# Which weight columns two early FFN products read, and waits for earlier stores on SyncE, in a gated mix of linear attention and a SwiGLU FFN

## The chip, the cores and the metric

The kernel runs on one core of one Trainium2 chip. The metric is the device time of an execution in microseconds (us). It is a little longer (1.2 to 1.8 us in the fast runs here) than the span that the profile shows, which goes from the first to the last instruction of the program on the core; how much longer turns out to matter here. A ratio is the mean time of one kernel's fast runs over that of the other kernel's fast runs of the same rounds, so it is not quite the ratio of the medians.

Names used below: PE is TensorE (matmuls), PEld its weight loads, DVE is VectorE, ACT is ScalarE, POOL is GpSimd, SyncE (SP) issues most DMAs. In the profile a line like L294 is a line of the kernel's text, usually that of a helper.

## The reference, cut to what matters

```python
# x: 2048 tokens x 640, bf16
g = sigmoid((x * gate_w).sum(-1, keepdims=True))
a = linear_attention(x, wqkv, w_phi, wo)      # 32 heads of 20, softmax features of q and k
b = (silu(x @ w_gate) * (x @ w_up)) @ w_down  # w_gate, w_up: 640 x 1728
return g * a + (1 - g) * b
```

The part under study is `x @ w_gate` and `x @ w_up`. The kernel computes them in products for 512 tokens and 128 of the 1728 columns.

## The kernel before

A long list of items, each a small unit of work, fixes the order in which every engine gets its instructions. `F0.8` is the FFN product for tokens 0 to 511 and columns 1024 to 1151 (column block 8). `K`, `V`, `Q` are projections of one tile of 128 tokens, `E` accumulates keys times values, `M` and `R` make projection weights, `D` is one output tile of 128 tokens, with its store. A tracker adds the semaphore waits that the reads and writes need.

```python
LOADS = """
x0 w0 x1 w1 x2 w2 x3 w3 w4 f0 h k0 k1 t4 k2 k3 k4 t5 ... t15 q0 q1 q2 q3
q4 f1 f2
"""
ORDER = """
... M1 i3 M0 F0.0 M2 V4 M3 M4 K0 K1 ...
R2 E5 K9 S8 P7 R1 E6 K10 S9 V12 P8 E7 P9 K11 S10 P10 F0.8 R3 F1.10 E8 E9 K12 E10 S11 S12 K14 S14
V11 K13 P11 P12 E11 K15 P14 R4 S13 P13 F1.9 S15 P15 E12 V13 T F1.8 ...
"""

FCUT = [0, 256, 896, F_FFN]      # columns of the three FFN loads f0, f1, f2

def load_ffn(c0, c1):            # all on SyncE's queue
    dma("sp", wg[:, :, c0:c1], B_w_gate[:, c0:c1].rearrange("(c p) j -> p c j", p=P))
    dma("sp", wu[:, :, c0:c1], B_w_up[:, c0:c1].rearrange("(c p) j -> p c j", p=P))

def fitem(bt, k):                # the FFN product: ten matmuls, one set of waits
    # ... (cut)
        mm(group(g, [(wg[:, c, P * k:P * k + P], xr[c]) for c in range(5)])
           + group(up, [(wu[:, c, P * k:P * k + P], xr[c]) for c in range(5)]))
    # ... (cut: ScalarE, VectorE and GpSimd make silu(gate) * up of it)

def ditem(bt, u):                # an output tile
    # ... (cut: 38 matmuls)
    o = osb[:, t % 4, :]
    if t < NT - 1:
        mm([p for ab in zip(*half) for p in ab])
        actop(o.rearrange("p (b c) -> p b c", b=2), halves(pr), ACTF.Copy, omg[:, t:t + 1])
        out_evs.append(dma("sp", out2[t * P:(t + 1) * P, :], o))
        return
    # ... (cut: the last tile goes out in three stores, two from SyncE and one from ScalarE)
# after the last item:
tr._wait("sp", dict(out_evs))    # SyncE waits until the stores have landed
```

The softmax here doesn't subtract the row's maximum and nothing guards it: scores larger than these inputs give would overflow.

## Time and profile before

| | before |
|---|---|
| time, median of the first 3 runs | 290.0 us (289.88 to 290.5) |
| span of the profiled run | 288.9 us |
| PE busy | 99% of the span |
| starts of back-to-back matmuls of 512 columns | 216 ns apart |

Back-to-back starts were 215.81 ns apart on average for 512 columns and 135.84 ns for 320 columns in this trace: 0.4165 ns a column, or N / 2.4 ns for N columns, and 2.5 ns besides. Start-to-start times less N / 2.4 ns give the holes in PE's stream.

The page of the kernel before. Each engine has its busy time, its share of the span and its number of instructions. The second line is a DMA queue that the page labels "instruction": number of packets within the span, MB, share of the DMA engines. The third is the chain of work that ended last, by engine.

```profile
PE 284.7 (99%) x1975; PEld 174.2 (60%) x1975; DVE 162.6 (56%) x243; ACT 148.1 (51%) x252; POOL 160.5 (56%) x125
...
q14 instruction: 6, 0.05, 0.1%
...
PE 93%; SPq 4%; DMA 2%; issue 0%; DVE 0%
```

PE is the bound: it is almost never idle and nearly all of the last chain is its own. The other engines matter only where PE waits for them.

The chain of waits of the kernel before, in order of time: start, length (us), what.

```profile
11.78 4.92 DMA wT<-in_A_wqkv_dram
...
16.75 34.89 PE ps L294 x344
51.64 0.58 issue
52.22 26.60 PE ps L294 x240
...
128.98 158.03 PE ps L294 x1020
...
287.03 0.32 DVE osb L719
```

The chain is PE work with few interruptions. The largest after the first 17 us is 0.58 us of "issue" at 51.64, which means: the profile does not see what PE waited for.

The timeline of PE around it: start, length (us), the merged instructions, and in brackets the idle time before them.

```profile
50.12 1.52 PE L294 MATMUL ps<-wqk,xT 128*128 128x320 bf16 x10
52.22 1.24 PE L294 MATMUL ps<-xT,wg 128*128 128x512 bf16 x5 [0.58 <-issue]
53.30 1.03 PE L294 MATMUL ps<-xT,wu 128*128 128x512 bf16 x4
```

PE stopped after a key projection (`K11`) and started again at 52.22 with the gate half of an FFN product, `F0.8`. A back-to-back start would have been at 51.47 (start of the last matmul of `K11`, 51.34, plus the 0.135 us that such matmuls of 320 columns are apart), so the hole is 0.75 us.

To find the cause, take the loads that `F0.8` needs. SyncE's timeline of the kernel before has the issues of the second and then the third FFN load (start, length):

```profile
37.70 0.58 SPq L348 DMA_DIRECT2D wg<-in_B_w_gate_dram  x1
38.33 0.52 SPq L348 DMA_DIRECT2D wu<-in_B_w_up_dram  x1
38.89 0.53 SPq L348 DMA_DIRECT2D wg<-in_B_w_gate_dram  x1
39.45 2.13 SPq L348 DMA_DIRECT2D wu<-in_B_w_up_dram  x1
```

The DMA view of the same kernel gives sizes and the time from issue to landing in us:

```profile
wg<-in_B_w_gate_dram SPq DMA_DIRECT2D x1, 1040.0 KB, 10.5
wu<-in_B_w_up_dram SPq DMA_DIRECT2D x1, 1040.0 KB, 12.7
wg<-in_B_w_gate_dram SPq DMA_DIRECT2D x1, 800.0 KB, 6.6
wu<-in_B_w_up_dram SPq DMA_DIRECT2D x1, 800.0 KB, 8.2
```

The 1040 KB loads are the third ones. Adding 39.45 and 12.7 puts the landing of the up half at 52.13 (the unrounded trace), which is 0.06 us before PE's first weight load and 0.09 us before its first matmul. The second load's up half landed at 38.33 + 8.2, or 46.57.

### The profile page before, as it was taken

Reading aid. Unit: us, or ns where it says so; the run is one execution under the profiler, and the core shown is the slowest. Engines: PE = TensorE matmul, PEld = TensorE weight load, DVE = VectorE, ACT = ScalarE, POOL = GpSimd, SP = SyncE. Lnnn points to the kernel's source line nnn. Section 1 sums busy time; section 2 is a strip of 40 time slices with the busy share of each in tenths; the row PEclk is TensorE's granted clock in tenths of the full one; section 3 lists DMA queues with packets and bytes.
Section 4 is the critical chain, followed back from the end, with each engine's and each line's share of the span. In section 5 each row is a group of like instructions: output and inputs, shape, how many; then the busy total and the mean of one; then the engine's idle time right before and its main releaser. Section 6 shows DMA issues by size and latency. Waiting matters only on the chain.

```text
span 288.9 us, 4883 instructions
## 1 busy us (share of the span) xinstructions
PE 284.7 (99%) x1975; PEld 174.2 (60%) x1975; DVE 162.6 (56%) x243; ACT 148.1 (51%) x252; POOL 160.5 (56%) x125
## 2 busy tenths in 40 slices
PE   7999999999999999999999999999999999999997
PEld 6667777575644445556775546675554446656776
DVE  2147748386468987769992285980316799200000
ACT  1478768576674556574354663224675452234112
POOL 8286899779544798844733347450663649601000
PEclk9999999999999999999999999999999999999999
DMA  7988689000010497302373102061020004410101
GB/s 216 173 121 129 119 230 338 7 2 1 0 49 0 75 331 133 71 11 40 63 133 93 20 1 50 2 133 58 2 50 0 2 1 82 93 45 0 48 23 48
DMA packets 48942, 21.61 MB, mean 75 GB/s; under 512 B 39384, under 2 KB 48792, under 8 KB 48920
## 3 DMA queue, kind: packets, MB, share of 16 engines
q1 hardware_dynamic: 48190, 20.62, 31.8%
q10 hardware_dynamic: 730, 0.68, 0.7%
q8 instruction: 16, 0.26, 0.4%
q14 instruction: 6, 0.05, 0.1%
HBM read 9.29 MB, written 2.62 MB: 41 GB/s over the span
## 4 chain that ended last, share of the span: by engine, by line
PE 93%; SPq 4%; DMA 2%; issue 0%; DVE 0%
PE ps L294 93%; SPq L347 2%; DMA wT<-in_A_wqkv_dram 2%; SPq L348 1%; DVE osb L719 0%; PE ps L306 0%
## 5 line engine op out<-in xcount | busy, mean ns | idle before, releaser
L322 POOL TENSOR_TENSOR hT<-hT,us 128x512 bf16<-128x512 bf16 (+1 forms) x56 | 65.7, 1182 | 66.9 <-DVE hT L326 66.7
L326 DVE SCALAR_TENSOR_TENSOR hT<-hT,ps 128x512 bf16<-128x512 bf16 (+1 forms) x56 | 37.6, 684 | 73.7 <-ACT hT L312 61.4
L294 PE MATMUL ps<-xT,wg 128*128 128x512 bf16 x260 | 64.6, 379 | 0.6 <-issue 0.6
L294 PE MATMUL ps<-xT,wu 128*128 128x512 bf16 x260 | 64.6, 379 | 0.0
L294 PE MATMUL ps<-wd,hT 128*128 128x320 bf16 (+2 forms) x462 | 63.9, 295 | 0.0
L312 ACT ACTIVATE hT<-ps 128x512 bf16<-128x512 f32 (+2 forms) x60 | 35.8, 596 | 47.3 <-PE ps L294 47.1
L322 POOL TENSOR_TENSOR ph<-eq,qc 128x1320 bf16<-128x1320 bf16 x16 | 42.4, 2647 | 26.1 <-DVE qc L632 24.0
L294 PEld LDWEIGHTS ps<-wd,hT 128*128 128x128 bf16 x462 | 44.5, 98 | 17.5 <-issue 0.2
L294 PE MATMUL ps<-wqk,xT 128*128 128x320 bf16 x320 | 47.7, 299 | 0.1
L294 PEld LDWEIGHTS ps<-xT,wu 128*128 128x128 bf16 x260 | 25.4, 98 | 30.7
L294 PEld LDWEIGHTS ps<-xT,wg 128*128 128x128 bf16 x260 | 25.0, 98 | 28.6 <-issue 0.9
L312 ACT ACTIVATE osb<-ps,omg 128x640 bf16<-128x640 f32 (+2 forms) x17 | 12.9, 758 | 53.7 <-PE ps L294 53.7
L322 POOL TENSOR_TENSOR ekr<-ekr,krec 128x1280 bf16<-128x1280 bf16 x16 | 37.4, 2358 | 4.9 <-DVE krec L336 4.9
L294 PEld LDWEIGHTS ps<-wqk,xT 128*128 128x128 bf16 x320 | 30.5, 98 | 13.2 <-ACT us L312 0.5
L312 ACT ACTIVATE us<-ps 128x512 bf16<-128x512 f32 (+1 forms) x56 | 33.2, 593 | 0.3 <-POOL hT L322 0.2
L312 ACT ACTIVATE eq<-ps 128x640 bf16<-128x640 f32 x32 | 22.4, 704 | 17.3 <-POOL ph L322 10.4
L333 DVE TENSOR_REDUCE ksum<-ekr 128x64 f32<-128x1280 bf16 x16 | 23.5, 1471 | 10.7 <-ACT ekr L312 10.7
L312 ACT ACTIVATE ekr<-ps 128x640 bf16<-128x640 f32 x32 | 22.3, 704 | 8.2 <-PE ps L294 7.7
L294 PE MATMUL ps<-wvg,xT 128*128 128x320 bf16 (+1 forms) x160 | 24.3, 300 | 0.7 <-DMA wvg<-in_A_wqkv_dram 0.6
L333 DVE TENSOR_REDUCE qz<-eq 128x64 f32<-128x1280 bf16 x16 | 23.7, 1479 | 2.2 <-ACT eq L312 2.2
L294 PE MATMUL ps<-wog,oT 128*128 128x320 bf16 (+2 forms) x165 | 24.7, 294 | 0.0
L333 DVE TENSOR_REDUCE qw<-ez 128x64 f32<-128x1280 bf16 x16 | 23.6, 1477 | 0.0
(73 smaller groups left out, 187.7 us busy)
## 6 DMA issues: line engine op xcount, KB each, us to landing
out_dram<-osb SPq DMA_DIRECT2D x15, 160.0 KB, 1.9
wd<-in_B_w_down_dram SPq DMA_DIRECT2D x1, 2080.0 KB, 10.5
wg<-in_B_w_gate_dram SPq DMA_DIRECT2D x1, 1040.0 KB, 10.5
wu<-in_B_w_up_dram SPq DMA_DIRECT2D x1, 1040.0 KB, 12.7
wg<-in_B_w_gate_dram SPq DMA_DIRECT2D x1, 800.0 KB, 6.6
wu<-in_B_w_up_dram SPq DMA_DIRECT2D x1, 800.0 KB, 8.2
wog<-in_A_wo_dram SPq DMA_DIRECT2D x2, 375.0 KB, 7.0
wvg<-in_A_wqkv_dram SPq DMA_DIRECT2D x4, 160.0 KB, 4.0
```

The lines of the kernel that those rows point to most:

```text
L294: last = pe.matmul(o, lhsT=l, rhs=r, start=st, stop=sp_, skip_group_check=sk)
L312: return run("act", lambda: act.activation(o, i, func, scale=scale), rd, [o])
L322: return run(e, lambda: eo.tensor_tensor(o, a, b, op), [a, b], [o])
L326: return run("dve", lambda: dve.scalar_tensor_tensor(out=o, in0=a, scalar=s, in1=b, op0=op0, op1=op1), rd, [o])
L333: return run("dve", lambda: dve.tensor_reduce(o, i, AX.X, ALU.add), [i], [o])
L347: return eo.dma_start_transpose(dst, src)
L348: return eo.dma_start(dst, src)
```

## The change

The intent: the first two FFN products among the keys take columns of the second load, which is there earlier, and the two products displaced go to their places later. Besides, before each store SyncE waits for the third and fourth last stores. The diff:

```diff
-R2 E5 K9 S8 P7 R1 E6 K10 S9 V12 P8 E7 P9 K11 S10 P10 F0.8 R3 F1.10 E8 E9 K12 E10 S11 S12 K14 S14
+R2 E5 K9 S8 P7 R1 E6 K10 S9 V12 P8 E7 P9 K11 S10 P10 F0.2 R3 F1.2 E8 E9 K12 E10 S11 S12 K14 S14
 ...
-Z J F0.9 F0.13 F1.13 A1 B1 B0 F1.2 F1.3 F1.0 C0 c0 B2 F0.3 F1.12 A2 C2 F0.2 F0.7 F0.12 L c2 Q3 A3
+Z J F0.9 F0.13 F1.13 A1 B1 B0 F1.10 F1.3 F1.0 C0 c0 B2 F0.3 F1.12 A2 C2 F0.8 F0.7 F0.12 L c2 Q3 A3
 ...
+    def stores_done():
+        for n, v in out_evs[-4:-2]:
+            sp.wait_ge(tr.sem[n], v)
+
 ...
             actop(o.rearrange("p (b c) -> p b c", b=2), halves(pr), ACTF.Copy, omg[:, t:t + 1])
+            stores_done()
             out_evs.append(dma("sp", out2[t * P:(t + 1) * P, :], o))
 ...
+            if e == "sp":
+                stores_done()
             out_evs.append(dma(e, out2[t * P:(t + 1) * P, c0:c1], o[:, c0:c1]))
```

## The prediction

> **What bounds the kernel now.** TensorE. By the page PE is busy 284.7 of 288.9 us (99%) at full granted clock, and the chain of work that ended last is 93% PE. Back-to-back 512-column matmuls start 216 ns apart (timeline). [...] So only holes in PE's stream can be won. Start-to-start time less N/2.4, matmul by matmul, shows one large hole after the first 5 us: 0.75 us at 51.5 us; after 17 us every other is 0.25 us or less.

> **What the hole is.** The chain of waits shows 0.58 us of "issue" at 51.64 (the modelled end of the matmul before), and the weight loads idle 0.89 us until 52.19. The instruction is the first matmul of F0.8, columns 1024 to 1151, from the third FFN load. Its ten matmuls share one set of waits, so it needs gate and up halves. Landings: second load 44.3 (wg) and 46.6 (wu); third load 49.4 and 52.13. PE resumes 0.06 us after the last. So PE waits for the third load, though the table of waits says "issue".

> **What the change does there.** F0.2 and F1.2 take columns 256 to 511: second load, landed 4.9 us before PE arrives (51.47). Work, shapes and PSUM rotation stay; F0.8 and F1.10 run later, when all has landed. The next user of the third load is F1.9, at 65.3. So PE should start the product about 0.75 us earlier.

> **Is it kept?** From 52.2 to the end PE's stream is unbroken but for holes of 0.1 to 0.25 us around the O items. GpSimd, VectorE and ScalarE mostly follow PE, so nearly all of the shift should reach the end. A little may return as a wait: GpSimd is busy without a break from 43.3 to 55.0 on key products, but the PE items after the FFN products use older keys.

> **The store waits.** They add two waits on SyncE before each of 17 stores. The third and fourth last stores were issued at least two D items before (5.2 us each; stores land in 1.1 to 3.0 us), so nearly all are met. A met wait should cost under 0.1 us (estimate: gaps between SyncE's DMA issues are about 0.04 us). In the tail ScalarE's store lands last (288.83), the last of SyncE at 288.25, so 0.1 us is hidden there too. Worth: 0. [...]

> **Predicted.** 290.0 - 0.75 is 289.25. The third load ends in a ragged tail (from 380 KB per us to under 40 in its last two), so unprofiled runs may have a smaller hole. I say 289.4 us, 288.9 to 290.0. Faster by over 2%: 0.01; within 2%: 0.98; slower: 0.01.

> **What would show it.** The idle before the first FFN product among the keys falls from 0.58 us to 0 and later PE work starts 0.7 us earlier; the third load still lands near 52; SyncE shows no new long wait; span about 288.2.

> **What would make it wrong.** The hole exists only under the profiler; a new wait on key products near 57 us or phi transposes near 127; stores held up by a slow landing.

## The result, and the profile after

| | before | after |
|---|---|---|
| median of 6 runs | 290.41 us (289.88 to 291.07) | 289.84 us (289.17 to 290.27) |
| ratio of the fast runs | | 0.9975, 95% interval 0.9954 to 0.9996 |
| span of the profiled run | 288.9 us | 288.4 us |
| its time less its span | 1.78 us | 1.24 us |

The gain is small, 0.7 us of the means. The last row is the surprise: the span accounts for 0.5 us of the two profiled runs' difference, and another 0.5 us lies outside it.

The page of the kernel after, with the lines shown of before:

```profile
PE 285.0 (99%) x1975; PEld 174.6 (61%) x1975; DVE 162.6 (56%) x243; ACT 148.2 (51%) x252; POOL 160.4 (56%) x125
...
q14 instruction: 7, 0.06, 0.1%
...
PE 93%; SPq 4%; DMA 2%; issue 0%; DVE 0%
```

PE is as busy and bounds the kernel as before. One line differs that nobody would look at: seven packets of queue 14 fell within the span instead of six.

The chain of waits of the kernel after:

```profile
14.36 4.61 DMA wT<-in_A_wqkv_dram
...
19.02 59.32 PE ps L294 x562
...
78.39 50.02 PE ps L294 x251
...
128.49 158.03 PE ps L294 x1020
...
286.54 0.32 DVE osb L724
```

The interruption at 51.6 is gone; PE's own work runs through from 19.02 to 78.34. But this run had another one: the chain hangs on a weight load that landed at 18.97, and PE stood there. By the start-to-start times of the matmuls (less N / 2.4 ns) that hole was 0.51 us in this run and none of before's at the same place; before had one of 0.24 us at 16.75. So the two profiles do not differ by the one hole alone.

The timeline of PE around the first FFN product among the keys, now `F0.2`:

```profile
50.38 1.52 PE L294 MATMUL ps<-wqk,xT 128*128 128x320 bf16 x10
51.74 1.24 PE L294 MATMUL ps<-xT,wg 128*128 128x512 bf16 x5
52.81 1.24 PE L294 MATMUL ps<-xT,wu 128*128 128x512 bf16 x5
```

There is no idle time in brackets any more. The start at 51.74 is 0.135 us after the last one of the projection. From this product's first matmul to the last matmul of the program PE took 234.56 us in both: after it nothing changed for PE.

SyncE's timeline and the DMA view of the kernel after:

```profile
39.85 2.58 SPq L348 DMA_DIRECT2D wg<-in_B_w_gate_dram  x1
42.47 0.53 SPq L348 DMA_DIRECT2D wu<-in_B_w_up_dram  x1
```

```profile
wg<-in_B_w_gate_dram SPq DMA_DIRECT2D x1, 1040.0 KB, 11.3
wu<-in_B_w_up_dram SPq DMA_DIRECT2D x1, 1040.0 KB, 11.5
wg<-in_B_w_gate_dram SPq DMA_DIRECT2D x1, 800.0 KB, 7.4
wu<-in_B_w_up_dram SPq DMA_DIRECT2D x1, 800.0 KB, 9.0
```

The third load's up half landed at 42.47 + 11.5, or 53.94 (unrounded trace), 1.8 us later than in the profile of before, because SyncE issued it later and for no reason that the change contains. With the old order PE would have stood 2.3 us in this run. So the hole is not a constant, and one profile does not give its size.

At last the waits of SyncE's own queue (us in total, times, longest), before:

```profile
SPq L348 <- ACT osb L312: 44.7, 11, 8.5
...
SPq L137 <- DMA out_dram<-osb: 1.7, 3, 0.9
```

and after:

```profile
SPq L137 <- ACT osb L312: 42.9, 10, 8.4
...
SPq L137 <- DMA out_dram<-osb: 1.7, 3, 0.9
```

The wait for ScalarE's results has only moved from the store's own instruction to the wait instruction ahead of it (L137 is the tracker's wait). The waits for stores are the same three, at the end of the program. So no store wait of the change was waited for.

### The profile page after: what moved, and what is told of

Read it like the earlier page. It is cut to its first block, busy times and chain, and to the rows that moved or that the text cites. A ratio compares the mean times of both kernels' runs of the same rounds, so it can differ in the third digit from the quotient of the medians.

```text
span 288.4 us, 4897 instructions
## 1 busy us (share of the span) xinstructions
PE 285.0 (99%) x1975; PEld 174.6 (61%) x1975; DVE 162.6 (56%) x243; ACT 148.2 (51%) x252; POOL 160.4 (56%) x125
## 4 chain that ended last, share of the span: by engine, by line
PE 93%; SPq 4%; DMA 2%; issue 0%; DVE 0%
PE ps L294 93%; SPq L347 3%; DMA wT<-in_A_wqkv_dram 2%; SPq L348 1%; DVE osb L724 0%; PE ps L306 0%
## 5 line engine op out<-in xcount | busy, mean ns | idle before, releaser
L312 ACT ACTIVATE hT<-ps 128x512 bf16<-128x512 f32 (+2 forms) x60 | 35.8, 596 | 46.6 <-PE ps L294 46.4
## 6 DMA issues: line engine op xcount, KB each, us to landing
wu<-in_B_w_up_dram SPq DMA_DIRECT2D x1, 1040.0 KB, 11.5
```

Of the source, the lines that this page charges most:

```text
L312: return run("act", lambda: act.activation(o, i, func, scale=scale), rd, [o])
```

## The experiments

Two theories were there at the start. The theory of the prediction: all of the gain is the hole at the third load, and the store waits are worth nothing. The rival: the store waits bring the gain or share in it.

An overview first. Times are means of the fast runs; "before" is the mean of the kernel before in the same rounds (11 runs). Executions over 1.5% slower than the fastest of the same kernel are left out of the means. The fifth column has the mean of each run's time less its own span. The three rounds ran on three chips (0, 8 and 9 on record), so means are compared within a round only.

| run | mean, us | before, us | ratio (95% interval) | less span, us |
|---|---|---|---|---|
| `a1_order_only` | 290.05 | 290.76 | 0.998 (0.9956 to 1.0005) | 1.77 |
| `a2_store_waits_only` | 289.83 | 290.76 | 0.9971 (0.9944 to 0.9998) | 1.23 |
| `a3_split_unit` | 290.18 | 290.76 | 0.9983 (0.9958 to 1.0008) | 1.78 |
| `a4_third_load_first` | 290.52 | 290.76 | 0.9995 (0.9967 to 1.0022) | 1.75 |
| `c1_before_again` | 290.74 | 290.90 | 0.9998 (0.9968 to 1.0027) | 1.77 |
| `c2_after_again` | 290.12 | 290.90 | 0.9981 (0.9943 to 1.0019) | 1.24 |
| `c3_store_waits_again` | 290.04 | 290.90 | 0.9974 (0.9941 to 1.0007) | 1.21 |
| `c4_wait_for_last_two_stores` | 290.73 | 290.90 | 0.9997 (0.9972 to 1.0023) | 1.24 |
| `d1_pad14` | 290.46 | 291.19 | 0.9975 (0.9945 to 1.0005) | 1.25 |
| `d2_pad128` | 291.12 | 291.19 | 0.9998 (0.9966 to 1.003) | 1.68 |
| `d3_f08_earlier` | 297.52 | 291.19 | 1.0218 (1.0185 to 1.0251) | 1.77 |
| `d4_wt_before_x4` | 290.96 | 291.19 | 0.9993 (0.9966 to 1.0019) | 1.21 |

The spread of the times, 289.8 to 292.6 us for the kernel before, makes every interval about half a percent wide. The effects are a few tenths of a percent. So the times alone decide little here, and the verdicts below rest on the traces and on the last column, whose single values stay within 0.06 us of the mean in each kernel. The spans of these runs are on record to 0.1 us only, which is most of that scatter: with the unrounded spans of the profiled runs it is 1.23 to 1.24 us for the seven with 93 or 95 SyncE instructions and 1.76 to 1.78 us for the six with 79.

### First round: each part alone, and two other ways to remove the hole

`a1_order_only` is the kernel before with the ORDER lines of the change.

> The kernel before with the new order alone, without the store waits. Theory (the whole gain is the hole before the first FFN product among the keys, where TensorE waited for the third FFN load): ratio 0.997 to 0.998 of before, as the whole change; PE idle before that product 0 instead of 0.58 us. Rival (the store waits bring the gain, or share in it): ratio 0.999 to 1.000.

The hole was gone, ratio 0.998, and the time less the span stayed at 1.77. Expected as such, but the interval still touches 1. In this run's profile the third load landed at 50.79 and PE arrived at 51.20, so the old order would have had no hole here either.

`a2_store_waits_only` is the kernel before with the `stores_done` lines of the change.

> The kernel before with the store waits alone, old order. Theory: ratio 1.000 within 0.1%; the hole before the first FFN product among the keys is still there, as long as the third load lands after 51.5 us; the stores issue and land as in before relative to the end of PE. Rival (store waits bring the gain): ratio 0.997 to 0.998.

The expectation failed: 0.9971, as good as the whole change. The profile was of no use, since its run fell into a strange state: it took 1064.97 us with PE at about a quarter of its pace from the start (512-column matmuls 840 ns apart, 216 in before), while the busy times of VectorE, ScalarE and GpSimd (157.0, 151.2 and 160.9 us) were about those of before. The granted clock of 1.0 that is listed for this run says nothing: its trace holds no clock record, and 1.0 is what is printed then. What brought this pace is not shown. The other five runs of this kernel were ordinary, and no other run did this.

`a3_split_unit` keeps the old order and lets the gate half of `F0.8` wait for the gate weights alone:

```diff
-            mm(group(g, ...) + group(up, ...))
+            gg, uu = group(g, ...), group(up, ...)
+            if (bt, k) == (0, 8):
+                mm(gg)
+                mm(uu)
+            else:
+                mm(gg + uu)
```

> The kernel before, old order and no store waits, but the first FFN product among the keys (F0.8) is issued as two units of five matmuls, so that the gate half waits for the gate weights alone. Theory (PE waits for the landing of the up half of the third load, because ten matmuls share one set of waits): the five gate matmuls start at once at about 51.5 us, and the hole shrinks by up to their 1.08 us: ratio about 0.997 to 0.9985, with what is left of the hole in front of the up half if that lands later than 52.5 us. Rival (the hole is the issue of the instruction or another resource, such as the PSUM pair): the hole of 0.58 us stays before the gate half, ratio 1.000.

Inconclusive: in its profile the whole third load had landed at 51.21, before PE arrived (51.30), so there was no hole to shrink.

`a4_third_load_first` is the old order with the two loads exchanged:

```diff
-q4 f1 f2
+q4 f2 f1
```

> The kernel before, old order and no store waits, but the third FFN load is issued ahead of the second. The columns that F0.8 and F1.10 take then land first. Theory (only the landing time of the columns matters): third load lands at about 45 (gate) and 47 to 48 us (up), hole gone, ratio 0.997 to 0.998 as the whole change; no new wait, since the second load's first user comes after 80 us. Rival (it matters which columns the product takes, for instance by where the weights lie): ratio 1.000 and the hole stays.

The trace did as expected: the issue-to-landing times of the two up halves changed places (the 1040 KB load is now the early one),

```profile
wu<-in_B_w_up_dram SPq DMA_DIRECT2D x1, 1040.0 KB, 8.9
...
wu<-in_B_w_up_dram SPq DMA_DIRECT2D x1, 800.0 KB, 10.7
```

the 1040 KB up half landed at 46.90, and PE had no hole at `F0.8`. The ratio, 0.9995, missed the expected 0.997 to 0.998. With times of this spread that neither supports nor refutes the size of the gain.

### Second round: a control, both kernels again, and a stronger store wait

`c1_before_again` is the kernel before, unchanged.

> A control: the kernel before, unchanged, run as a candidate against itself. Ratio 1.000 by construction; the interval and any offset show how far the place in the round and run-to-run spread (289.8 to 292.0 us so far) can fake a gain. If it comes out at 0.997 to 0.998, part of every gain so far is such an offset. Theory of the hole: if the third load lands after 51.5 us in the profiled run, PE stands until 0.06 us after the landing; if it lands earlier, there is no hole.

0.9998: no gain from the place in the round shows, but the half-width of the interval, 0.3%, is as large as the effect. Its profile had a small hole: the third load landed at 51.57, PE started at 51.66.

`c2_after_again` is the whole change, unchanged.

> The whole change again, beside the control in the same rounds. Theory (hole of 0.75 us on average, between 0 and 2.3 us from run to run): mean 0.5 to 1.0 us under the control's, and a narrower spread, since the variable hole is gone. Rival (the gain was an offset of the comparison): same mean as the control.

Its mean was 0.6 us under the control's and 0.8 us under before's. The expected narrower spread did not show (289.16 to 292.04). So the hole is not the main cause of the spread.

`c3_store_waits_again` is the same kernel as `a2_store_waits_only`.

> The store waits alone again (the first try gave 0.9971, with a profile that fell in a run of 1065 us). Theory: as the control within 0.3 us, the first ratio being the offset and the spread; the stores at the end issue at the same distance from the last matmul as before (within 0.1 us). Rival (the store waits gain 0.5 to 0.8 us by themselves): 0.5 to 0.8 us under the control, and something in the trace that is shorter.

Again 0.9974, against the theory. Its span, 288.35, was no shorter than the control's, 288.32, and its hole at `F0.8` was there (landing 51.61, start 51.70). The stores at the end stood as before relative to PE. So whatever the store waits gain is not in the span. Putting time less span beside each kernel showed it at once: 1.18 to 1.27 us for every fast run with the store waits, 1.73 to 1.82 us for every run without them.

`c4_wait_for_last_two_stores` is the whole change with a stronger wait:

```diff
-        for n, v in out_evs[-4:-2]:
+        for n, v in out_evs[-2:]:
```

> The whole change, but SyncE waits for the last two stores instead of the third and fourth last: the dose of the store wait raised until it binds. Theory: the waits of the change are always met because stores are 5.2 us apart and land in 1.1 to 3 us; only in the tail can this stronger wait bind: the last SyncE store then waits for the one before it (landed 2.5 to 3 us after its issue), issues about 1.2 us later than in the whole change and lands about 0.5 to 0.9 us after the present end. Expected: 0.4 to 1.0 us over the whole change. Rival (store waits cost or gain something at each of 17 stores): a change spread over the run, visible as moved PE work before the last product.

Here the waits bind, as SyncE's waits show in this run (compare 1.7 us in three waits above):

```profile
SPq L137 <- DMA out_dram<-osb: 6.3, 4, 3.3
SPq L348 <- DMA out_dram<-osb: 2.1, 1, 2.1
```

The last store from SyncE waited 2.1 us for the one before it, and the span ended 3.62 us after the start of the last matmul; in before, after and the control it ended 2.10 us after. That costs 1.5 us, more than the 0.5 to 0.9 us expected of the store itself. PE was not touched. In time the kernel was about 0.6 us over the whole change of the same rounds (1.1 us by the medians, as one run of the whole change took 292.04 us). What is late is SyncE's next issue: by the views above the waits sit on SyncE's own queue, 6.3 us in four waits and 2.1 us in one.

### What the time outside the span is

The trace also keeps what is recorded around the span: DMA packets of the instruction queue and semaphore updates, among them one sweep over some 230 semaphores after the last instruction. This is an extract of the traces, in us from the span's start:

```
run                          SyncE    last 8192-byte packet   end of   first update    time less
                             instr.   on queue 14 at          span     of the sweep    span (this run)
before                         79       289.96                288.88   289.67 (+0.79)   1.78
a1_order_only                  79       289.11                288.03   288.82 (+0.79)   1.78
c1_before_again                79       289.66                288.32   289.10 (+0.78)   1.76
after                          93       268.08                288.40   288.64 (+0.24)   1.24
c2_after_again                 93       267.59                288.22   288.47 (+0.25)   1.24
c3_store_waits_again           93       267.72                288.35   288.60 (+0.24)   1.24
c4_wait_for_last_two_stores    95       258.32                289.32   289.57 (+0.25)   1.24
```

Without the store waits the last packet of queue 14 comes about 1.1 us after the span's end, and the sweep starts 0.54 us later after the span than it does with them. The page labels queue 14 "instruction" (7 packets within the span in after), and queue 8 as well. That this packet carries instructions of SyncE is inferred from the label and from its moving with SyncE's instruction count.

Inside the span the same cost can be seen on a single store. From the end of ScalarE's instruction to SyncE's issue of the store it took, in us, for the ninth to the seventeenth store:

```
before                       1.05 0.03 0.03 0.03 0.03 0.03 0.03 0.03 0.03
after                        1.12 0.10 0.10 0.52 0.09 0.08 0.08 0.08 0.08
c3_store_waits_again         1.12 0.10 0.10 0.52 0.08 0.08 0.08 0.08 0.08
c4_wait_for_last_two_stores  1.12 0.10 0.52 0.08 0.08 0.08 0.08 0.08 2.06
```

The store waits cost 0.05 us per store, and exactly one store costs 0.44 us more, the one that the late packet follows. With two more instructions (the last row) it is the store before it. So there is a point in SyncE's instruction stream where it loses about half a microsecond, and a packet on queue 14 follows (in `after` the 80th instruction starts at 267.14 and the packet at 268.08). Counting SyncE's instructions in the traces gives the point exactly: in `after`, `c3` and `c4` the loss lies between the 79th and the 80th of the program. The kernel before has just 79, so there the point lies behind the last wait, where nothing hides it and the sweep starts later by as much. With the store waits the 80th instruction is the issue of a store, at a time when SyncE has 5 us between stores.

New theory: the gain outside the span comes from the 14 more instructions on SyncE, whatever they wait for. Rival: from waiting for stores.

### Third round: the instruction count, the dose of the hole, and an attempt to do better

`d1_pad14` is the kernel before with 14 wait instructions (two waits each) on an early load, all issued at one place (from 39.9 us in its trace; 42 us was expected), where SyncE has nothing to do:

```diff
-    for w in LOADS.split() + ORDER.split():
+    for i, w in enumerate(LOADS.split() + ORDER.split()):
+        if i == len(LOADS.split()):
+            for _ in range(28):
+                sp.wait_ge(tr.sem["d0"], 16)
         ops[w[0]](*[int(a) for a in w[1:].split(".") if a])
```

> The kernel before (old order, no store waits), plus 14 SyncE wait instructions on a load that landed long before, all at about 42 us, where SyncE has nothing to do. So far every run with store waits took 1.24 us more than its span, every run without them 1.77 us, and the late instruction fetch (8 KB on queue 14) fell at 258 to 268 us with them, but 1.1 us after the end of the span without them. New theory (the 14 extra instructions move the point where SyncE's instruction stream enters its next block from the time after the last store to a time when SyncE is idle; the stores do not matter): time less span 1.24 us, late fetch between 255 and 275 us, first semaphore reset 0.25 us after the span's end. Rival (waiting for the stores themselves shortens the end): 1.77 us, fetch and resets as before.

`d2_pad128` is the same with `range(256)`, so 128 instructions. That 128 are one block was the author's estimate; no run had shown it by then.

> The same with 128 wait instructions[...]. New theory: the block boundary is again just after the last wait of the program: time less span back at 1.77 us, the last fetch after the end of the span. Rival (any extra wait instruction helps, or it is the number of instructions): 1.24 us or less.

Extract of the traces as above:

```
d1_pad14                       93       242.59                289.35   289.59 (+0.24)   time less span 1.21 to 1.29
d2_pad128                     207       289.98                288.96   289.69 (+0.73)   time less span 1.65 to 1.73
```

```profile
q8 instruction: 16, 0.26, 0.4%
q14 instruction: 6, 0.05, 0.1%
```

and the 16 packets of queue 8 are of 16384 bytes each. At the 64 bytes estimated above they would hold 4096 instructions. Only PE, with 3950 matmuls and weight loads, has about so many (about 247 a packet); that the queue is PE's is inferred from this.

`d2_pad128` has the old order, and its profile shows the hole of the kernel before once more:

```profile
50.16 1.52 PE L294 MATMUL ps<-wqk,xT 128*128 128x320 bf16 x10
52.30 1.24 PE L294 MATMUL ps<-xT,wg 128*128 128x512 bf16 x5 [0.62 <-issue]
```

The up half landed at 52.22, and PE started 0.08 us later.

`d3_f08_earlier` raises the dose of the hole:

```diff
-... K10 S9 V12 P8 E7 P9 K11 S10 P10 F0.8 R3 F1.10 ...
+... K10 S9 F0.8 V12 P8 E7 P9 K11 S10 P10 R3 F1.10 ...
```

> The kernel before (old order, no store waits), but F0.8 is issued two projections and one accumulation earlier, where TensorE arrives at about 48.4 us. The dose of the third load's hole. Theory: PE stands until 0.09 us after the landing of the third load's up half (50.8 to 53.9 us in the profiles so far, mean 51.7), so a hole of about 3.3 us (2.4 to 5.5), and the span is 2.4 to 3.4 us longer than before's mean, ratio 1.008 to 1.012; what follows the hole runs at its old pace to the end (234.6 us from the product to the last matmul, plus the 3.1 us of PE work that now stands behind it). Rival (the hole does not follow the landing, or later slack absorbs it): ratio under 1.004.

PE arrived at 48.50, the up half landed at 53.40, PE started 0.09 us later: a hole of 5.0 us, within the range expected.

```profile
47.14 1.52 PE L294 MATMUL ps<-wqk,xT 128*128 128x320 bf16 x10
53.49 2.29 PE L294 MATMUL ps<-xT,wg 128*128 128x512 bf16 x5 [4.83 <-issue]
55.58 1.90 PE L294 MATMUL ps<-xT,wu 128*128 128x512 bf16 x5
```

But the end was 8.2 us later than in the profile of before, and the mean of the runs 6.3 us over before's, twice what was expected. Two things were missing in the expectation. First, the eight starts after that of the first matmul behind the hole were 381 ns (once) and about 426 ns (seven times) apart instead of 216, 1.7 us in all: each group of five above took 2.29 or 1.90 us instead of 1.24. The idle time before was 4.83 us, and the trace's clock records have half of the clock for 3.41 us from 53.48 us on. On the page of this run that is the 7 in the row of the granted clock (tenths of full speed, 40 slices of the span):

```profile
PEclk9999999799999999999999999999999999999999
```

Second, the chain of waits then ran through GpSimd (`ekr` is a key product that the next `E` item needs), where PE stood another 1.55 us and 0.60 us:

```profile
58.91 1.15 POOL hT L322
60.06 4.14 POOL ekr L322 x2
...
64.66 2.37 POOL ekr L322
...
67.07 19.93 PE ps L294 x182
```

With `F0.8` moved ahead, GpSimd's product of the FFN (at 58.91) stood before the key products (from 60.06) in the program, as it did in the trace, and they came late. The sum, 5.0 + 1.7 + 1.55 + 0.60 less the 0.75 of before's own hole, is 8.1 us of the 8.2.

`d4_wt_before_x4` is the whole change with an earlier place for the loads behind the holes at 16 to 19 us:

```diff
-x0 w0 ... f0 h k0 k1 t4 k2 k3 k4 t5 ...
+x0 w0 ... f0 h k0 k1 k2 k3 k4 t4 t5 ...
-... M0 F0.0 M2 V4 M3 M4 K0 ...
+... M0 F0.0 M2 M3 V4 M4 K0 ...
```

> A try at beating both: the whole change, with the five transposed key-weight loads ahead of the fifth token tile's load, and the fourth weight product ahead of that tile's value product. It aims at the holes of 0.24 to 0.51 us at 16 to 19 us, where PE waited for the landing of those weights in before and after. Theory (PE's stream is all there is): holes there gone, 0.2 us less than the whole change on average, 1.0 to 1.2 us less than before: ratio 0.996 to 0.997. It may be lost in the spread of the runs, or the tile's load may now be the one waited for.

It failed. The wait for the weights went, and a larger one for the displaced token tile came. This is the table of waits of that run for 9 to 22 us:

```profile
PE ps L294 <- DMA xT<-in_A_x_dram: 1.0, 1, 1.0
```

By start-to-start times PE lost 1.12 us there, more than the 0.24 to 0.51 us it was to save. No version here is shown to be better than the change.

## Why the prediction was right or wrong

**The time was right; of its two terms one was too large and the other was wrongly zero.** The predicted 289.4 us (288.9 to 290.0) holds the measured median of 289.84, and "within 2%" is true. The predicted gain was 0.6 us, and the measured one 0.7 us of the means. The prediction derived it from the hole alone. That the number fits is in part luck: a hole taken as 0.75 us, about 0.27 us too large on average, stood in for a gain of 0.53 us at the end that was not foreseen. The level was 0.4 us off besides, as the 290.0 us of before, a median of three, became 290.41 us with six.

**"PE waits for the third load."** Right, and shown. In all five profiles in which PE was held by this load, its first start came 0.08 to 0.09 us after the landing of the up half:

| profiled run (old order) | landing | PE ready | PE starts | hole |
|---|---|---|---|---|
| before | 52.13 | 51.47 | 52.22 | 0.75 |
| `c1_before_again` | 51.57 | 51.55 | 51.66 | 0.11 |
| `c3_store_waits_again` | 51.61 | 51.61 | 51.70 | 0.09 |
| `d2_pad128` | 52.22 | 51.52 | 52.30 | 0.78 |
| `d3_f08_earlier` (moved earlier) | 53.40 | 48.50 | 53.49 | 5.00 |
| `d1_pad14` | 51.38 | 52.62 | 52.62 | 0 |

**"So PE should start the product about 0.75 us earlier."** The mechanism was right, the size was not: 0.75 us was the hole of one run. The landing moved between 50.8 and 53.9 us, and PE's arrival between 51.1 and 52.6. Take the ten profiles whose stream up to there is that of before: before, after, those of the first two rounds and the two padded kernels, without `a4_third_load_first` (its loads were exchanged) and `a2_store_waits_only` (slow). The hole, or what it would have been with the old order (landing + 0.09 less the time at which PE was ready), is 0.75 (before), 2.29 (after), 0 (`a1`), 0 (`a3`), 0.11 (`c1`), 0.27 (`c2`), 0.09 (`c3`), 0.46 (`c4`), 0 (`d1`) and 0.78 (`d2`): 0.48 us on average. This is an estimate from ten executions, with half of it from a single one. The timings of the order alone (0.998, interval to 1.0005) agree with it but cannot prove it.

**"Nearly all of the shift should reach the end."** Right. From that product's first matmul to the last one of the program PE took 234.56 us in all twelve profiles other than `d3` and the slow `a2`, hole or not. `d3` shows that this holds only while the order on GpSimd stays and PE does not fall to half pace behind the hole, as it did there for 3.41 us behind 4.83 us of idle time.

**"The store waits. ... Worth: 0."** This step failed. The first half was right: the waits are met and cost 0.05 us per store (predicted under 0.1 a wait), and nothing waits for them; stores landed 1.5 to 3.0 us after the start of their issue in before (1.1 us after its end for the fastest). But the prediction counted only what a wait instruction does while it waits. That the 14 instructions move the half microsecond that SyncE loses behind its 79th instruction to a place among its stores was not on the list. The runs showed 0.53 us of gain, outside the span, in every run that has them; fourteen waits on something else gave the same, and 128 gave almost none of it.

**"The third load still lands near 52"; "span about 288.2".** In the profile after it landed at 53.94, and the span was 288.4, because of a hole of 0.51 us at 19 us that has nothing to do with the change.

**The sum.** The hole's 0.48 and the end's 0.53 make about 1.0 us; measured were 0.7 us (first comparison) and 0.8 us (second). Both intervals contain 1.0. The spread between runs, which has other sources, hides the difference. One of them is visible in the profiles: the number of matmuls that ran at half pace at the beginning (in before those of 128 columns started 107 ns apart, later 56) was 22 in before and 43 in `d1_pad14`, whose 51st matmul started 1.4 us later (8.27 against 6.85; `d1_pad14` had a span of 289.35 us without any hole at `F0.8`). The times alone do not show the order's part at all: in the second round the store waits alone (290.04 us) came out no slower than the whole change (290.12 us). That part rests on the traces.

**What stays open.** What SyncE does in the half microsecond at the block's end is not seen in these traces; that the loss belongs to the block's end is inferred from its staying behind the 79th instruction while the program around it moved, from the repeat after 128, and from the packet that follows it each time (0.94 us after the 80th instruction's start in `after`). How many bytes an instruction takes is not shown beyond the estimate of 64. Why `d2_pad128` kept 0.08 us is open. Whether the split unit (`a3`) would shrink a hole was not tested, as its profiled run had none. What moves the landing of the third load by 3 us from run to run is open too.

## What to carry to other kernels

Where one engine is 99% busy, list its start-to-start holes and set each against the landing of every load that the stalled instruction needs; an "issue" in a table of waits may be a DMA. Such a hole is a race between a load and a stream, so take its size from several profiles, and prefer data that lands with several microseconds to spare, as here the second load does (landed at 46.57, PE ready at 51.47). And compare time less span between kernels: added or removed instructions on a queue can change the end of the program although nothing waits for them (14 of them on SyncE took 0.53 us off it here).
